# S4 of pair 6 by accumulating DMA, with its product moved behind product 5 of pair 7

## The chip, the cores and the metric

One Trainium2 chip, one core. The metric is the device time in microseconds (us) of one execution. Ratios are the mean time of one kernel's runs over that of the other's runs of the same rounds, so not quite the ratio of the medians that are quoted.

## The reference, cut to what matters

```python
xn = _layernorm(x)                       # 2048 x 512
return x + ssm(xn, ...) + swiglu(xn, w1, w3, w2)
# ssm:    h[t] = Lam_bar * h[t-1] + Bu[t];  y = 2 Re(h C^T) + xn * Dskip
# swiglu: (silu(xn w1) * (xn w3)) w2
```

The kernel joins the last product of both branches. The gated activations (14 tiles of 128) and the states (8 tiles, real and imaginary) stand side by side in the tile `act`, and one matrix product with w2 and C gives the output. This product is done with seven block products in place of eight (the scheme of Strassen and Winograd): the tokens are taken in eight pairs of chunks of 128, n = 0 to 7, and each pair has the left blocks a11, a12, a21, a22 and the sums S1 to S4 of them.

## The kernel before

Each product is eleven matmuls of 128x128 by 128x256. The sums are made in fp16. S2 and S3 lie in a place shared by the even pairs and one shared by the odd ones; S1 = a21 + a22 replaces a21. S4 = a12 + S2 replaces a12, so it can only be made after product 2 has read a12.

```python
LATER = (4, 5)          # pairs whose product 3 runs in the next pair, behind product 5
...
def product2():
    mms(f, v["a12"], weight(1, D1), False)
    v["s4"] = v["a12"]
    if n in (2, 3, 4, 5):
        gp.dma_start(out=v["s4"], in_=v["s2"], accum_op=ALU.add)      # L1094
    else:
        bg.own(0.85, -1.1)
        nc.vector.tensor_tensor(out=v["s4"], in0=v["a12"], in1=v["s2"], op=ALU.add)   # L1097
    add(o1[:, D1], f, o1[:, D1])                                      # L1066
...
def product3():
    for t, cols in halves:
        mms(t, v["s4"], weight(1, D2), False, cols)
        add(o1[:, right(cols)], t, q0[:, cols])
    ...                                                                # store of o1
...
# order of the products in pairs 4 to 7: 1, 4, 2, 6, 5, 7, 3
if i == 3 and n in LATER:
    later[n] = product3
else:
    products[i - 1]()
if i == 5 and n - 1 in later:
    later.pop(n - 1)()
    if n + 1 < len(pairs):
        seeds(n + 1)
if n in LATER:
    bg.fill()
```

`bg` is a queue of VectorE work (state columns, sums S1 to S3 of the next pair). Behind most products (`bg.fill()`), and in the pairs of `LATER` behind every one, it hands out as much as a rough model of VectorE's lead over TensorE allows. In the profile, L1055 is every matmul of the seven products, L525 the last step of a block of state columns, L1001 the sums S3 and S2, L1006 S1, L1140 the addition of product 7, L1072 the stores.

Of the kernel before, what the change touches and what calls it, by code (L numbers as in the profile page):

```python
# [14 lines left out]
FP32 = DT.float32  # L15
# [48 lines left out]
def kernel(  # L64
# [31 lines left out]
    NG = 3  # L96
    TH = TBLK // 2
    LEAD = 1.7
    LATER = (4, 5)
    AHEAD = (MID, 8, 1, None)  # L100
    NWARM = 10
    DH = D // 2
# [48 lines left out]
    x_blk = [x_all[:, i] for i in range(NBLK)]  # L151
# [805 lines left out]
    def weight(kh, dsl, half=False):  # L957
        gates = [w2_sb[:, kh * NFH + k, dsl] for k in range(NFH)]
        return [v.bitcast(FP16) if half else v for v in gates] + [weight_state(kh, dsl)[:, k, :]
                                                                   for k in range(2 * NPH)]  # L960
# [22 lines left out]
    def sum_homes():  # L983
        n = NK * P
        spare = tw[:, 3, :, :].rearrange("p k d -> p (k d)")
        xs = [x_blk[i].rearrange("p c d -> p (c d)") for i in range(2)]
        both = x_all[:, 0:2].rearrange("p b c d -> p b (c d)")[:, :, n:n + 2 * DH].bitcast(FP32)
        q = [const.tile([P, DH], FP32, name="q0"), both[:, 1, :], both[:, 0, :], both]
        return [[v[:, 0:n] for v in xs], [spare[:, 0:n], spare[:, n:2 * n]]], q
# [24 lines left out]
    def seeds(n):  # L1014
        b, p = pairs[n]
        bg.flush(("res", b))
        if n in (0, 3, 5, 7):
            f, e = (ps_bu.tile([P, TBLK], FP32, name="bu_ps") for _ in range(2))
            g, z = (ps_y.tile([P, D], FP32, name="y_ps") for _ in range(2))
        else:  # L1020
            f, e, z, g = (ps_gu.tile([P, TBLK], FP32, name="gu_ps") for _ in range(4))
        g, e, f, z = (t[:, 0:DH] for t in (g, e, f, z))
        o2 = xn_blk[b][:, 2 * p + 1, :]
        if n == len(pairs) - 1:
            spare = ps_gu.tile([P, TBLK], FP32, name="gu_ps")
            halves = [(t[:, 0:DH // 2], slice(i * DH // 2, (i + 1) * DH // 2)) for i, t in enumerate((e, spare))]
        else:
            halves = [(e, slice(0, DH))]
        nc.scalar.activation(out=z, in_=o2[:, D1], func=ACT.Copy)
        for t, cols in halves:  # L1030
            nc.scalar.activation(out=t, in_=o2[:, DH + cols.start:DH + cols.stop], func=ACT.Copy)
        seeded[n] = g, halves, f, z
# [4 lines left out]
    def y_fast(n, then=(), between=()):  # L1037
        b, p = pairs[n]
# [7 lines left out]
        v = sums[n]  # L1046
        res = xn_blk[b]
        g, halves, f, z = seeded[n]
        q0 = x_blk[2].rearrange("p c d -> p (c d)")[:, 0:2 * DH].bitcast(FP32) if n == 5 else q[0]
        tsum = [weight(0, D2, True)] + [[tw[:, i, k, :] for k in range(NK)] for i in range(3)]  # L1050
        o1, o2 = res[:, c1, :], res[:, c1 + 1, :]

        def mms(out, left, right, start, cols=slice(0, DH)):
            for k in range(NK):
                nc.tensor.matmul(out=out, lhsT=left[:, k, :], rhs=right[k][:, cols],  # L1055
                                 start=(start and k == 0), stop=(k == NK - 1), skip_group_check=True)
            bg.tensor(1.2 * (cols.stop - cols.start) / DH)

        def steps():
            if b == 0:  # L1060
                sin_step()
                sin_step()

        def add(out, x, w):
            bg.own(0.35)
            nc.vector.tensor_tensor(out=out, in0=x, in1=w, op=ALU.add)  # L1066

        def store(cl, o, dsl=slice(0, D), eng=nc.sync):
            if b == 0:
                held.append((cl, o))  # L1070
            else:
                eng.dma_start(out=ov[:, b * CPB + cl, dsl], in_=o[:, dsl])  # L1072
# [15 lines left out]
        def product2():  # L1088
            if b == 0:
                bg.first(list(then))  # L1090
            mms(f, v["a12"], weight(1, D1), False)
            v["s4"] = v["a12"]
            if n in (2, 3, 4, 5):
                gp.dma_start(out=v["s4"], in_=v["s2"], accum_op=ALU.add)  # L1094
            else:
                bg.own(0.85, -1.1)
                nc.vector.tensor_tensor(out=v["s4"], in0=v["a12"], in1=v["s2"], op=ALU.add)  # L1097
            add(o1[:, D1], f, o1[:, D1])
            if last:
                store(c1, o1, D1)  # L1100
            if n + 1 < len(pairs) and n not in (1, 2, 3) and n - 1 not in LATER:
                seeds(n + 1)
            steps()
# [13 lines left out]
        def product4():  # L1117
            mms(z, v["a22"], tsum[3], False)
            copy(q[2], z)
            steps()  # L1120
            bg.fill(1.2 if b > 0 and n not in LATER else None)

# [14 lines left out]
        def product7():  # L1137
# [5 lines left out]
            if b == 0:  # L1143
                steps()
                bg.fill()

        products = (product1, product2, product3, product4, product5, product6, product7)
        for i in ((1, 5, 2, 6, 4, 3, 7) if b == 0 else (1, 2, 4, 6, 5, 7, 3) if b == 1 else ORDER.get(n, (1, 4, 2, 6, 5, 7, 3))):
# [10 lines that stand above are left out]
# [24 lines left out]
    homes, q = sum_homes()  # L1183
# [36 lines left out]
    bg.flush(("sums", 0))  # L1220
    keep_ends(0)
    y_fast(0, row_sums(1, *pairs[1]))
    ln_scalar_engine(3, lambda cl: ps_y.tile([P, D], FP32, name="y_ps"), sins, (0, 2, 5))
    y_fast(1)
    sin_step(("norm", 2, CPB - 1))
    for cl, o in held:
# [10 lines left out]
    last_posts = ssm_tasks(3, between=[(0.0, after_y2, None), *row_sums(4, *pairs[4])])  # L1237
    keep_ends(1)
    y_fast(2, row_sums(3, *pairs[3]), bu_fast(3, 0))
    y_done.append(2)  # L1240
    y_fast(3, (), bu_fast(3, 1))
# [42 lines left out]
```

## Time and profile before

| | before |
|---|---|
| median of 3 runs | 200.99 us (200.81 to 201.39) |
| span of the profiled run | 198.9 us |
| TensorE busy | 195.2 us, 98% |
| VectorE busy | 182.2 us, 92% |
| four last pairs, first to last matmul | 162.49 to 196.19, 33.70 us |

### The profile page before, as it was taken

To read this page: it belongs to the slowest core of one execution; us is meant where nothing else is said; L and a number is where in the kernel's file an instruction comes from. 1 tells how busy PE (TensorE), PEld (TensorE's weight loads), DVE (VectorE), ACT (ScalarE), POOL (GpSimd) and SP (SyncE) were. 2 spreads that over 40 slices of the span, in tenths; PEclk is the share of its full clock that TensorE was granted. 3 is DMA by queue.
4 is the path that set the end of the run, shared out by engine and by line. 5 is a ranking of instruction groups with operands and counts; after the bars stand their busy time and mean duration, and the time that the engine had idled before them with its cause. 6 is when DMAs were issued, how large, how long until landed. Compare 5 with 4: busy or idle time off the path is not lost.

```text
span 198.9 us, 3703 instructions
## 1 busy us (share of the span) xinstructions
PE 195.2 (98%) x1401; PEld 130.7 (66%) x1401; DVE 182.2 (92%) x257; ACT 135.0 (68%) x281; POOL 50.9 (26%) x75
## 2 busy tenths in 40 slices
PE   8999999999999999999999999999999999999994
PEld 2874444444444488856555478888566678888893
DVE  3699699999999999989999997999999999999972
ACT  4899797799999987968998684362688782111220
POOL 7170289700411134041202305040021303300000
PEclk9999999999999999999999999999999999999999
DMA  5999999992497054730997546838147723941111
GB/s 154 319 240 185 328 200 98 348 280 46 70 181 141 0 105 82 135 106 0 164 154 107 100 83 108 169 84 124 53 64 134 143 52 57 170 96 33 53 40 44
DMA packets 32258, 25.12 MB, mean 126 GB/s; under 512 B 16240, under 2 KB 29936, under 8 KB 32240
## 3 DMA queue, kind: packets, MB, share of 16 engines
q0 software_dynamic: 6128, 11.38, 33.6%
q1 hardware_dynamic: 25536, 13.21, 28.2%
q10 hardware_dynamic: 576, 0.30, 0.5%
q8 instruction: 11, 0.18, 0.4%
q14 instruction: 7, 0.06, 0.1%
HBM read 7.74 MB, written 2.10 MB: 49 GB/s over the span
## 4 chain that ended last, share of the span: by engine, by line
PE 96%; DMA 1%; DVE 1%; issue 0%
PE gu_ps L587 34%; PE gu_ps L1055 18%; PE y_ps L1055 10%; PE gu_ps L849 7%; PE bu_ps L1055 7%; PE y_ps L454 3%; PE bu_ps L454 3%; PE y_ps L870 3%; PE y_ps L781 3%; PE gu_ps L619 2%; PE gu_ps L781 2%; PE bu_ps L781 1%; PE bu_ps L870 1%; DMA x_blk<-in_A_x_dram 1%; PE bu_ps L619 1%; PE y_ps L243 1%
## 5 line engine op out<-in xcount | busy, mean ns | idle before, releaser
L587 PE MATMUL gu_ps<-xnT,w_sb 128*128 128x512 bf16 x312 | 69.6, 379 | 0.0
L587 PEld LDWEIGHTS <-w_sb 128*128 128x128 bf16 x312 | 30.5, 98 | 34.2
L1055 PEld LDWEIGHTS <-act 128*128 128x128 f16 x462 | 43.5, 98 | 5.4
L596 ACT ACTIVATE g<-gu_ps 128x512 bf16<-128x512 f32 x41 | 24.8, 606 | 5.9 <-PE gu_ps L587 3.5
L597 ACT ACTIVATE u<-gu_ps 128x512 bf16<-128x512 f32 x41 | 24.9, 606 | 4.4 <-PE gu_ps L587 4.1
L505 DVE TENSOR_TENSOR_SCAN u<-rho,ends,u 128x512 bf16<-128x512 f32 x16 | 20.0, 1271 | 0.0
L527 POOL DMA_DIRECT2D act<-p x7 | 9.2, 1321 | 34.1 <-DVE act L519 22.1
L1055 PE MATMUL gu_ps<-w_sb,act 128*128 128x256 bf16 (+3 forms) x126 | 16.0, 267 | 0.0
L849 PE MATMUL gu_ps<-xnT,w_sb 128*128 128x512 bf16 x64 | 15.9, 379 | 0.0
L604 DVE TENSOR_TENSOR act<-g,u 128x1024 f16<-128x1024 bf16 x21 | 14.3, 680 | 0.0
L861 ACT ACTIVATE g<-gu_ps 128x512 bf16<-128x512 f32 x14 | 8.4, 599 | 5.4 <-PE gu_ps L849 5.0
L454 PEld LDWEIGHTS <-bt 128*128 128x128 bf16 x64 | 6.3, 98 | 7.5
L1078 ACT ACTIVATE x_blk<-gu_ps 128x256 f32<-128x256 f32 (+1 forms) x9 | 3.3, 368 | 10.6 <-PE gu_ps L1055 10.6
L1055 PE MATMUL bu_ps<-w_sb,act 128*128 128x256 bf16 (+3 forms) x84 | 10.4, 264 | 0.0
L1055 PE MATMUL gu_ps<-ct,act 128*128 128x256 f16 (+1 forms) x72 | 10.4, 267 | 0.0
L849 PEld LDWEIGHTS <-w_sb 128*128 128x128 bf16 x64 | 6.3, 98 | 4.8
L505 DVE TENSOR_TENSOR_SCAN u<-rho,u 128x512 bf16<-128x512 f32 x8 | 9.2, 1207 | 0.0
L1055 PEld LDWEIGHTS <-x_blk 128*128 128x128 f16 x88 | 8.6, 98 | 1.0
L1055 PEld LDWEIGHTS <-tw 128*128 128x128 f16 x88 | 8.6, 98 | 1.0
L513 DVE TENSOR_TENSOR p<-u,tabe 128x2048 f16<-128x2048 bf16 (+1 forms) x8 | 8.7, 1086 | 0.1
L519 DVE TENSOR_TENSOR act<-u,tabe 128x2048 f16<-128x2048 bf16 (+1 forms) x8 | 8.7, 1085 | 0.0
L488 DVE TENSOR_TENSOR u<-u,tabe 128x2048 bf16<-128x2048 bf16 x7 | 8.5, 1220 | 0.1
(203 smaller groups left out, 392.5 us busy)
## 6 DMA issues: line engine op xcount, KB each, us to landing
act<-p POOLq DMA_DIRECT2D x6, 512.0 KB, 6.1
xn<-x_blk POOLq DMA_DIRECT2D x4, 512.0 KB, 5.5
out_dram<-xn SPq DMA_DIRECT2D x15, 128.0 KB, 1.7
w_sb<-in_B_w_dram SPq DMA_DIRECT2D x1, 1792.0 KB, 8.2
act<-act POOLq DMA_DIRECT2D x5, 352.0 KB, 4.6
w_sb<-in_B_w_dram SPq DMA_DIRECT2D x2, 768.0 KB, 6.1
u<-p POOLq DMA_DIRECT2D x3, 512.0 KB, 5.2
w_sb<-in_B_w_dram SPq DMA_DIRECT2D x4, 256.0 KB, 4.4
```

Of the source, the lines that this page charges most:

```text
L454: nc.tensor.matmul(out=ps, lhsT=bt[:, ri, dt, pt * P:(pt + 1) * P], rhs=xnT_blk[b][:, dt, :], start=(dt == 0), stop=(dt == NDT - 1))
L505: nc.vector.tensor_tensor_scan(out=v, data0=rho[:, pt:pt + 1].to_broadcast([P, TBLK]), data1=v, initial=init, op0=ALU.mult, op1=ALU.add)
L513: nc.vector.tensor_tensor(out=by_state(st["p16"][:, csl]), in0=by_chunk(st["g"][:, :, ::-1, tsl]), in1=by_chunk(tabe[:, psl, 2:0:-1, tsl]) ...
L519: nc.vector.tensor_tensor(out=by_state(act_state(b, hf)[:, csl]), in0=by_chunk(st["g"][:, :, :, tsl]), in1=by_chunk(tabe[:, psl, 0:1, tsl] ...
L527: gp.dma_start(out=a, in_=p16, accum_op=ALU.add)
L587: nc.tensor.matmul(out=ps[:, tsl], lhsT=w[:, dt, f * P:(f + 1) * P], rhs=xnT[:, dt, tsl], start=(dt == 0), stop=(dt == NDT - 1))
L596: nc.scalar.activation(out=g16[:, f % 2, :], in_=g_ps, func=ACT.Silu)
L597: nc.scalar.activation(out=u16[:, f % 2, :], in_=u_ps, func=ACT.Copy)
L604: nc.vector.tensor_tensor(out=act_gates(b, f - 1), in0=split(g16), in1=split(u16), op=ALU.mult)
L781: nc.tensor.matmul(out=out[:, h * TH:(h + 1) * TH], lhsT=left[:, h, k, :], rhs=right[:, k, :], start=(start and h == 0 and k == 0), stop=( ...
L849: nc.tensor.matmul(out=ps, lhsT=w[:, dt, f * P:(f + 1) * P], rhs=xnT[:, dt, :], start=(dt == 0), stop=(dt == NDT - 1))
L1055: nc.tensor.matmul(out=out, lhsT=left[:, k, :], rhs=right[k][:, cols], start=(start and k == 0), stop=(k == NK - 1), skip_group_check=True)
```

## The change

The intent is to take the addition of S4 in pair 6 (128x1408, 0.89 us) off VectorE, which idles only 0.32 us there, and to let the DMA engines do it. The transfer takes longer than the addition, so product 3 of pair 6, which reads S4, is put off until behind product 5 of pair 7. Its addend q0 must live longer, so pair 7 writes its own into an idle buffer. Because pair 6 now stands in `LATER`, its calls to the VectorE queue change too (the code above).

```diff
-    LATER = (4, 5)
+    LATER = (4, 5, 6)
...
-        q0 = x_blk[2]...bitcast(FP32) if n == 5 else q[0]
+        q0 = x_blk[2]...bitcast(FP32) if n in (5, 7) else q[0]
...
-            if n in (2, 3, 4, 5):
+            if n in (2, 3, 4, 5, 6):
                 gp.dma_start(out=v["s4"], in_=v["s2"], accum_op=ALU.add)
```

More of the change, by code (lines that the diff above doesn't have):

```diff
@@ L1048, in y_fast @@
         g, halves, f, z = seeded[n]
-        q0 = x_blk[2].rearrange("p c d -> p (c d)")[:, 0:2 * DH].bitcast(FP32) if n == 5 else q[0]
+        q0 = x_blk[2].rearrange("p c d -> p (c d)")[:, 0:2 * DH].bitcast(FP32) if n in (5, 7) else q[0]
         tsum = [weight(0, D2, True)] + [[tw[:, i, k, :] for k in range(NK)] for i in range(3)]
```

## The prediction

> **What bounds the kernel now.** I read the page first: which engine is busy, and what the chain that ended last consists of.
>
> ```profile
> PE 195.2 (98%) x1401; PEld 130.7 (66%) x1401; DVE 182.2 (92%) x257; ACT 135.0 (68%) x281; POOL 50.9 (26%) x75
> PEclk9999999999999999999999999999999999999999
> PE 96%; DMA 1%; DVE 1%; issue 0%
> ```
>
> TensorE fills 98% of the span at the full clock, and 96% of the chain is TensorE's own work. VectorE has 92%, so it is the engine that could become a second bound. A busy matmul row alone doesn't prove that nothing is lost, so I read the chain of waits over the stretch that the change touches, from the first product of pair 4 on (each pair of token chunks has seven products, of eleven matmuls each):
>
> ```profile
> 162.49 7.21 PE gu_ps L1055 x66
> 169.70 2.40 PE y_ps L1055 x22
> 172.10 1.20 PE bu_ps L1055 x11
> ...
> 191.31 1.20 PE y_ps L1055 x11
> 192.52 0.61 PE bu_ps L1055 x11
> 193.13 0.61 PE gu_ps L1055 x11
> 193.74 1.20 PE y_ps L1055 x11
> 194.94 0.61 PE bu_ps L1055 x11
> 195.56 0.63 PE gu_ps L1055 x11
> 196.19 0.02 issue
> 196.21 0.29 DVE xn L1066
> ```
>
> Every piece starts where the one before it ends, and no other engine stands in the chain until 196.19. Four pairs of seven products are 28; 28 x 1.20 = 33.6 us, and 196.19 - 162.49 = 33.70 us. So TensorE waits for nothing in this whole stretch: there is no wait here for the change to remove. Behind it stand 198.9 - 196.2 = 2.7 us: two additions on half tiles, three last stores, and the end of the program.
>
> The change lightens VectorE, so I asked how it stands there. The timeline of VectorE in pair 6 and at the start of pair 7 (start, duration, line):
>
> ```profile
> 181.80 0.89 DVE L1097 TENSOR_TENSOR act<-act,x_blk 128x1408 f16<-128x1408 f16 x1
> ...
> 187.75 0.42 DVE L1066 TENSOR_TENSOR xn<-gu_ps,q 128x256 bf16<-128x256 f32 x1 [0.32 <-PE gu_ps L1055]
> 188.09 0.68 DVE L525 TENSOR_TENSOR act<-act,p 128x1024 f16<-128x1024 f16 x1
> 188.69 0.89 DVE L1001 TENSOR_TENSOR tw<-act 128x1408 f16<-128x1408 f16 x1
> 189.61 0.89 DVE L1001 TENSOR_TENSOR tw<-tw,act 128x1408 f16<-128x1408 f16 x1
> 190.42 0.88 DVE L1006 TENSOR_TENSOR act<-act 128x1408 f16<-128x1408 f16 x1
> 191.35 0.89 DVE L1097 TENSOR_TENSOR act<-act,tw 128x1408 f16<-128x1408 f16 x1
> ```
>
> The first line is S4 of pair 6, which the change takes away; the last is S4 of pair 7, which stays. Between them lies the preparation of pair 7: its last state columns (L525) and its sums S3, S2, S1. They come in time, though not by much. Product 4 of pair 7 starts at 188.75 and comes to its state columns with its eighth matmul, 7 x 0.109 us later; with 0.1 us for the weight load it needs L525 at about 189.4, and L525 ends at 188.77: 0.6 us to spare. Product 6 of pair 7 needs S2 at about 191.05, and S2 ends at 190.50: 0.5 us.
>
> **What the Trainium skill says.** "DMA: Bandwidth & Descriptors", Rules for kernel authors: a DMA that accumulates is to be issued from GpSimd, as here. Its section on the anatomy of one DMA on the GpSimd path fits about 2.0 us plus bytes/436e3; for 352 KB (360,448 bytes) that is 2.8 us as an estimate from that page. The trace shows 3.8 us for the same transfer in pairs 4 and 5 (L1094), and I use that. The same rules warn that an accumulating DMA must not overlap another access of the same bytes. In this kernel the issue waits for the product that reads them: product 2 of pair 4 ends at 165.93 and the issue starts at 166.40, product 2 of pair 5 ends at 173.14 and the issue starts at 173.60, so about 0.47 us behind it. "Perfetto Trace Analysis", Identifying the Most-Contended Engine, says that matmul busy time is no measure of the distance to roofline; it is why I rested the bound on the gapless chain and on 28 x 1.20, not on the 98%.
>
> **The change part by part.**
>
> 1. It removes one addition of 128x1408 from VectorE in pair 6: 0.89 us by the row above (0.80 until the next instruction starts). TensorE doesn't wait for VectorE there, so the path gets nothing of it: 0.
>
> 2. It adds one accumulating DMA. Product 2 of pair 6 ends at 181.54, so the issue starts near 182.0, takes GpSimd 0.9 us, and lands after 3.8 us: near 185.8, or 186.7 if counted from the end of the issue. GpSimd has nothing after 174.5, and the DMA engines are nearly idle (12% in 176.9 to 184.1, by the table of stretches). Product 3 of pair 6 wants the result at 186.35 in the old order: that would be too tight, which is why it is moved along. In the new order it runs after product 5 of pair 7, at about 192.4: over 5 us to spare. Cost on the path: 0.
>
> 3. It moves product 3 of pair 6 by six products. The number of matmuls stays, 28 products. Product 7 of pair 6 then ends at 186.35 and pair 7 starts there instead of at 187.55: its products 1, 4, 2, 6, 5 come 1.20 us earlier (186.35, 187.55, 188.75, 189.95, 191.15), product 3 of pair 6 fills 192.35 to 193.57, and product 7 and the two halves of product 3 of pair 7 start at 193.6 and 194.8 as before. If nothing waits, the last matmul ends at 196.2 again.
>
> 4. So the inputs of pair 7 are due 1.20 us earlier. VectorE gets back 0.80 us (S4) and, as the addition behind product 3 moves away, 0.42 us with 0.32 us of waiting. Suppose the worst order of the instructions, the old one. The addition of product 7 of pair 6 (0.69 us, 0.60 to the next start) can't start before 186.35 + 0.2. Then L525 runs 187.15 to 187.83, against a need at about 188.2: 0.4 us to spare. S3 runs to 188.6, S2 to about 189.5 against 189.85: 0.35 us. S1 ends near 190.3 against 191.05. It just fits. The changed calls to the queue of VectorE work should make it better: behind product 4 its limit goes from 1.2 to 1.7, each product of pair 6 gets another call, and the model no longer charges 0.85 us for S4, so state columns and S3 should be handed out before the addition of product 7. I expect about 1 us to spare or more. Cost: 0, at worst a few tenths.
>
> 5. The other output buffer of product 6 (q0 in the idle x_blk) keeps the old value alive and costs nothing. The accumulator of product 3 of pair 6 stays occupied longer; the spare tile of pair 7 comes around to the accumulator of product 2, which is free by 183.0.
>
> 6. The store of the row of product 3 (128 KB, 1.7 us to landing) moves from about 188.2 to 194.2 and should land near 195.9. The last stores are issued at 195.77, near 196.0 and at 196.53, so it is out of their way: 0 to 0.2 us.
>
> Sum: 0 saved, 0 to 0.2 us added. From 200.99 us I predict 201.0.
>
> **The rivals.**
>
> *A wait takes its place.* If L525 or S2 comes late, TensorE stops in product 4 or 6 of pair 7. For: VectorE is busy 7.17 of 7.20 us in pair 6 and the spare time falls from 0.6 and 0.5 to 0.4 and 0.35 in the worst order. Against: it is relieved of more than it is pressed by. It would make 201.2 to 201.8.
>
> *The end gets crowded.* Another 128 KB comes into the last 5 us. For: the stores after 195.77 end the program, and the 64 KB store issued at 192.61 took 3.5 us instead of 1.7. If the moved store does so, it lands at 197.7 and may hold back the others by some tenths: 201.2 to 201.5. Against: the last store of 32 KB still lands later, at 198.0.
>
> *A gain after all.* If the VectorE relief let the last products come earlier, it would be up to 0.9 us: 200.1. For: VectorE at 92%. Against: TensorE has no gap to close in the stretch, and the last addition waits for the last matmul (0.27 us of idle in front of it), not for VectorE's queue. I hold it for nearly excluded.
>
> *The accumulation lands late.* It would need a landing after 192.4, thus over 10 us instead of 3.8. The slowest row of accumulating transfers in the table of issues has 6.1 us (512 KB). Excluded.
>
> **Range and chances.** The three runs of before spread over 200.81 to 201.39, so half a microsecond either way is noise. The losses that I can name are a few tenths; the gains are smaller. The range is 200.5 to 201.6. Two per cent would be 4 us: for that, TensorE would have to stand still for three whole products, or lose as many, and nothing points to it. Faster 0.01, within 2% 0.97, slower 0.02.
>
> **What would show it.** In the changed profile: one 128x1408 addition fewer in L1097 and one issue more in L1094, near 182.0, landing near 186. The chain from 162.5 to 196.2 still of TensorE alone, with the gu_ps product of pair 6 behind a bu_ps and gu_ps half. VectorE with a longer idle piece before 195, since its work of pair 7 is done earlier. L525 and S2 ahead of their products by about 1 us. The step 4 is wrong if TensorE shows a wait on VectorE near 188 or 190; step 6 if the time from the last addition to the end of the span grows over 2.4 us. The whole is wrong if the last matmul ends more than half a microsecond away from 196.2.

## The result, and the profile after

The changed kernel takes 200.97 us (median of 4 runs, 200.91 to 201.34) against 201.01 us (4 runs) of the kernel before. The ratio is 0.9999, with a 95% interval of 0.998 to 1.0018: the same time.

From the page of the changed kernel, busy time and instructions of each engine:

```profile
PE 194.9 (98%) x1401; PEld 130.7 (66%) x1401; DVE 181.3 (91%) x256; ACT 135.0 (68%) x281; POOL 51.5 (26%) x76
```

VectorE has one instruction and 0.9 us less, GpSimd one issue more; TensorE has its 1401 matmuls as before. The chain of waits of the changed kernel over the last four pairs (start, duration, what):

```profile
162.72 7.20 PE gu_ps L1055 x66
...
191.54 0.61 PE bu_ps L1055 x11
192.15 1.81 PE gu_ps L1055 x22
193.97 1.20 PE y_ps L1055 x11
...
196.41 0.02 issue
196.44 0.29 DVE xn L1066
```

The piece of 1.81 us at 192.15 is a half of product 5 of pair 7 (0.61) and then product 3 of pair 6 (1.20), in its new place. Still every piece begins where the last one ends: 196.41 - 162.72 = 33.69 us, against 33.70. The whole stretch lies 0.23 us later than before. That comes from the start of the kernel, which the change doesn't touch: in the chains, the long piece on L587 begins at 12.44 in the kernel before and at 12.67 in the changed one. TensorE waits 0.2 us there in the kernel before (L243 on the first normalized chunk), and in the changed kernel, by the view of who waited for whom (us in total, times, longest):

```profile
PE y_ps L243 <- DVE xn L224: 0.5, 1, 0.5
PE gu_ps L619 <- DMA w_sb<-in_B_w_dram: 0.2, 1, 0.2
```

These are arrivals of the first inputs and weights. They differ from run to run (the stretch begins between 162.45 and 162.84 in the ten profiles), by 0.4 us or 0.2% of the time; differences of 0.1% between kernels below are smaller than that.

The timeline of VectorE in the changed kernel, pair 6 and the start of pair 7:

```profile
186.03 0.68 DVE L525 TENSOR_TENSOR act<-act,p 128x1024 f16<-128x1024 f16 x1
186.84 0.69 DVE L1140 TENSOR_TENSOR xn<-gu_ps,x_blk 128x512 bf16<-128x512 f32 x1
187.45 0.88 DVE L1001 TENSOR_TENSOR tw<-act 128x1408 f16<-128x1408 f16 x1
188.37 0.89 DVE L1001 TENSOR_TENSOR tw<-tw,act 128x1408 f16<-128x1408 f16 x1
189.17 0.88 DVE L1006 TENSOR_TENSOR act<-act 128x1408 f16<-128x1408 f16 x1
190.38 0.89 DVE L1097 TENSOR_TENSOR act<-act,tw 128x1408 f16<-128x1408 f16 x1 [0.32 <-PE bu_ps L1055]
```

L525 is now handed out ahead of L1140, and the last addition shown, S4 of pair 7, waits for TensorE (0.32 us), where in the kernel before it followed without a gap. The products 4 and 6 of pair 7, which read L525 and S2 (the second L1001), in the kernel before and then in the changed one:

```profile
188.75 1.36 PE L1055 MATMUL y_ps<-tw,act 128*128 128x256 f16 x11
191.15 1.36 PE L1055 MATMUL y_ps<-tw 128*128 128x256 f16 x11
...
187.77 1.36 PE L1055 MATMUL y_ps<-tw,act 128*128 128x256 f16 x11
190.18 1.36 PE L1055 MATMUL y_ps<-tw 128*128 128x256 f16 x11
```

S2 ends 0.65 us ahead of its product before the change (189.61 + 0.89 against 191.15) and 0.92 us ahead after it (188.37 + 0.89 against 190.18). The issue of the transfer on GpSimd, and its row in the table of issues (KB each, us to landing):

```profile
182.24 0.86 POOL L1094 DMA_DIRECT2D act<-x_blk  x1 [7.50 <-DVE xn L949]
...
act<-x_blk POOLq DMA_DIRECT2D x1, 352.0 KB, 3.8
```

Product 2 of pair 6 ends at 181.77 and the issue follows 0.47 us later, landing near 186.0. (The wait is put down to L949, which ended just before; the 0.47 us behind product 2 are the same as in pairs 4 and 5.)

### The profile page after: what moved, and what is told of

The parts are those of the page before. It is cut to its first block, busy times and chain, and to the rows that moved or that the text cites. A ratio compares the mean times of both kernels' runs of the same rounds, so it can differ in the third digit from the quotient of the medians.

```text
span 199.1 us, 3703 instructions
## 1 busy us (share of the span) xinstructions
PE 194.9 (98%) x1401; PEld 130.7 (66%) x1401; DVE 181.3 (91%) x256; ACT 135.0 (68%) x281; POOL 51.5 (26%) x76
## 4 chain that ended last, share of the span: by engine, by line
PE 95%; DMA 2%; SPq 1%; issue 0%; DVE 0%
PE gu_ps L587 34%; PE gu_ps L1055 18%; PE y_ps L1055 10%; PE gu_ps L849 7%; PE bu_ps L1055 7%; PE bu_ps L454 3%; PE y_ps L454 3%; PE y_ps L870 3%; PE y_ps L781 3%; DMA w_sb<-in_B_w_dram 2%; PE gu_ps L619 2%; PE gu_ps L781 2%; PE bu_ps L781 1%; PE bu_ps L870 1%; PE bu_ps L619 1%; SPq L166 0%
## 5 line engine op out<-in xcount | busy, mean ns | idle before, releaser
L587 PE MATMUL gu_ps<-xnT,w_sb 128*128 128x512 bf16 x312 | 69.6, 379 | 0.0
L587 PEld LDWEIGHTS <-w_sb 128*128 128x128 bf16 x312 | 30.5, 98 | 34.2
```

Source lines behind the costliest of these rows:

```text
L587: nc.tensor.matmul(out=ps[:, tsl], lhsT=w[:, dt, f * P:(f + 1) * P], rhs=xnT[:, dt, tsl], start=(dt == 0), stop=(dt == NDT - 1))
```

## The experiments

Eight kernels ran on one chip, the first four of them held against 11 runs of the kernel before (median 201.16 us), the others against the same 11 and one more (201.18 us), so that a drift between the two groups would not show in the intervals of the second. The changed kernel was measured apart from them, its ratio is to the 4 runs of the kernel before of its own rounds (201.01 us). What each left in its one trace, with "spare" for the time from the end of VectorE's instruction to the start of the matmul that reads it (S2: product 6 of pair 7; L525: the eighth matmul of product 4 of pair 7, its start plus 7 x 0.109 us):

| kernel | ratio of times to before (95%) | four pairs | spare S2 | spare L525 |
|---|---|---|---|---|
| before | 1 | 33.70 | 0.65 | 0.74 |
| changed | 0.9999 (0.998 to 1.0018) | 33.69 | 0.92 | 1.82 |
| DMA alone | 1.0008 (0.9989 to 1.0028) | 33.69 | 0.94 | 1.96 |
| move alone | 0.9992 (0.9975 to 1.0009) | 33.69 | 0.19 | 0.28 |
| before, 2 loads | 1.0033 (1.0018 to 1.0048) | 34.41 | | waits |
| changed, 2 loads | 1.0027 (1.0012 to 1.0041) | 34.35 | waits | |
| move alone, 1 load | 1.0027 (1.0013 to 1.0041) | 34.35 | | waits |
| changed, 1 load | 0.9985 (0.9972 to 0.9998) | 33.69 | 0.34 | 1.02 |
| before without product 3 of pair 6 | 0.9949 (0.9936 to 0.9962) | 32.70 | | |
| changed, store held back | 1.0008 (0.9996 to 1.0021) | 33.69 | | |

The four pairs are the difference of two starts in one chain, so they show a tenth of a microsecond where the times alone don't. "Changed, 1 load" is a warning: its time lies just clear of 1, below it, while its stretch is the same to 0.01 us. A difference of 0.15% in the times is no proof of anything here.

### The DMA alone

```diff
-            if n in (2, 3, 4, 5):
+            if n in (2, 3, 4, 5, 6):        # LATER stays (4, 5)
```

> The kernel before with S4 of pair 6 by accumulating DMA, product 3 of pair 6 in its old place, straight behind product 7 of pair 6. Theory (TensorE sets the end, VectorE's relief is worth nothing): the transfer is issued near 182.0 and lands near 185.8, its product wants its weights near 186.25, so it just fits, by about 0.4 us: the time stays at 201.0, or TensorE waits 0.1 to 0.5 us on the DMA at the start of that product and the time is up to 201.5. Rival A (the removed VectorE addition is worth its 0.8 us and the deferral gives it away): 200.2. Rival B (a transfer without the deferral is late): a wait of over 1 us before product 3 of pair 6, 202 or more.

Measured: 201.13 us, no wait of TensorE in the stretch. The issue stands at 182.36, so the landing is at 186.2, and product 3 of pair 6 starts at 186.69. It fits by half a microsecond. The 3.8 us count from the start of the issue: counted from its end, 183.22, the landing would be at 187.0, and TensorE would have waited. The first matmuls of that product, with no idling in front of them in brackets:

```profile
186.69 0.93 PE L1055 MATMUL gu_ps<-w_sb,act 128*128 128x256 bf16 x7
```

Rivals A and B fall: lightening VectorE by 0.8 us brings no time, and the deferral was not needed in this run to have the transfer in time. My prediction had called this place "too tight"; it was tight, and held. VectorE turns part of the relief into waiting: it stands still for 0.73 us in front of the addition of product 6 of pair 6.

### The move alone

```diff
-            if n in (2, 3, 4, 5, 6):        # LATER = (4, 5, 6) stays
+            if n in (2, 3, 4, 5):
```

> The changed kernel with S4 of pair 6 back on VectorE: only product 3 is moved. VectorE then has the old work, and pair 7 is due 1.20 us earlier. Theory: the spare time of the state columns (L525) and of S2 in front of pair 7, measured in the changed kernel at 1.7 and 0.8 us with the addition gone, falls to 0.1 to 0.2 us, just enough: 201.0, with at most 0.3 us of waiting of TensorE in products 4 or 6 of pair 7. Rival A (the VectorE addition costs its 0.8 us on the path wherever it runs): 201.8 against the changed kernel. Rival C (moving the product costs something at the end, by the store): the end lies later by the same 0.1 to 0.2 us as in the changed kernel, with the last matmul at the same distance from the first product of pair 4 (33.7 us).

Measured: 200.85 us and 33.69 us. VectorE's S2, and product 6 of pair 7 that reads it:

```profile
189.06 0.89 DVE L1001 TENSOR_TENSOR tw<-tw,act 128x1408 f16<-128x1408 f16 x1
...
190.14 1.36 PE L1055 MATMUL y_ps<-tw 128*128 128x256 f16 x11
```

S2 ends at 189.95 and is read at 190.14. The move alone fits with 0.19 us left, as expected; Rival A (0.8 us lost) falls. So does Rival C: from the start of the last addition to the end of the span it is 2.7 us here as in the kernel before. So neither half of the change costs time and neither saves any that these runs show; what they move is the spare time of S2, from 0.65 to 0.94 us (DMA) and to 0.19 us (move).

### Two more additions in both kernels

To see whether this spare time is real, VectorE got work that nothing reads, at the place of S4 of pair 6, with two additions here and one in the two runs after:

```diff
+            if n == 6:
+                dead = bt_flat[:, 2 * TBLK:2 * TBLK + NK * P].bitcast(FP16)
+                for _ in range(2):
+                    nc.vector.tensor_tensor(out=dead, in0=dead, in1=dead, op=ALU.subtract)
             add(o1[:, D1], f, o1[:, D1])
```

The model of the queue is not told of this work.

> The kernel before with two more VectorE additions of 128x1408 on dead data behind S4 of pair 6 (about 1.6 us more). Theory: VectorE has 0.32 us of idling and 0.6 us of spare time in front of pair 7, so 1.6 us is more than it can hide: L525 comes near 190.0 instead of 188.8, TensorE waits 0.6 to 0.8 us in product 4 of pair 7 and the time is 201.7. Rival A (VectorE's queue is the bound): plus the whole 1.6 us, 202.6. Rival D (there is much more spare time): 201.0.

> The changed kernel with the same two more additions at the same place in pair 6. Theory by the measured spare time of the changed kernel: S2 ends 0.8 us before product 6 of pair 7 needs it, and VectorE idles 0.13 us in front of L1140, so TensorE waits 0.6 to 0.8 us in front of product 6: 201.7, about as much as in the kernel before with the same load. That would mean that the change bought no spare time at this spot: what it takes from VectorE it asks back by bringing pair 7 forward by one product. Rival (the change buys the 0.8 us of the removed addition as spare time): at most 0.1 us of waiting, 201.0, while the kernel before with the same load has 201.7.

Measured: 201.79 us and 201.70 us. The two additions in the kernel before, and the instruction behind them:

```profile
182.84 1.81 DVE L1101 TENSOR_TENSOR bt<-bt 128x1408 f16<-128x1408 f16 x2
184.57 0.42 DVE L1066 TENSOR_TENSOR xn<-gu_ps,xn 128x256 bf16<-128x256 f32 x1
```

So the load is 1.73 us from start to start. The waits in the kernel before with the load, and in the changed kernel with it (matmuls in order of time; the brackets give TensorE's idling and who ended it):

```profile
188.99 0.93 PE L1055 MATMUL y_ps<-tw,act 128*128 128x256 f16 x7
190.36 0.61 PE L1055 MATMUL y_ps<-tw,act 128*128 128x256 f16 x4 [0.44 <-DVE act L525]
```

```profile
185.49 1.36 PE L1055 MATMUL gu_ps<-tw,x_blk 128*128 128x256 f16 x11 [0.22 <-DVE q L1066]
...
190.55 1.38 PE L1055 MATMUL y_ps<-tw 128*128 128x256 f16 x11
```

In the kernel before, product 4 of pair 7 does its seven matmuls on the gated activations and then stops for the state columns, as the prediction had located it. The stretch grows by 0.71 us: of 1.73 us of load, about 1.0 us disappears, which is near the spare 0.74 us of L525 and the 0.32 us of idling together. Rival A (the whole load) and Rival D (none of it) fall. In the changed kernel it grows by 0.66 us. The size is as expected, the place only in part: counted from the start of the stretch, product 6 of pair 7 comes 0.64 us later than without the load (S2 ends at 190.49), but 0.39 us of that are lost already in front of product 7 of pair 6, which waits until VectorE has read the accumulator that it goes on with. I had not seen this wait coming; it stems from the order of the changed kernel, in which two more steps of state columns stand ahead of that addition (L1066 at 183.56 in the changed kernel without load).

So the changed kernel bears hardly more of this load than the kernel before: the rival, in which the change buys 0.8 us, falls.

### One more addition, with S4 on VectorE or on the DMA

> Product 3 of pair 6 moved, its S4 on VectorE, and one more addition of 128x1408 on dead data behind it (0.8 us more). In the run with the move alone S2 ended 0.1 us before product 6 of pair 7 took it, and L525 0.2 us before product 4 did. Theory (the move uses up VectorE's spare time, the transfer of S4 to the DMA gives it back): nothing is left to hide the load, TensorE waits 0.6 to 0.8 us in products 4 and 6 of pair 7, stretch of the four pairs 34.3 to 34.5 us instead of 33.7, time 201.7. Rival (the load is hidden as long as VectorE idles anywhere behind it): 201.0.

> The changed kernel with one such addition at the same place: VectorE has then just the work that it has with the move alone, but in the order of the changed kernel. Theory: S2 comes 0.67 us later than in the changed kernel and is taken 0.1 us later: at most 0.1 us of waiting, stretch 33.7 to 33.8 us, time 201.0. With the run before this one (same load, S4 on VectorE, 0.7 us of waiting expected) it would show that the DMA's half of the change is worth one addition of spare time and no time. Rival (the DMA's transfer slows VectorE or TensorE at this place): a wait of 0.3 us or more.

Measured: 201.76 us with S4 on VectorE and 200.91 us with S4 on the DMA; stretches of 34.35 and 33.69 us. The wait of the former, and the same product of the latter, undivided and without a wait:

```profile
189.21 0.61 PE L1055 MATMUL y_ps<-tw,act 128*128 128x256 f16 x4 [0.39 <-DVE act L525]
...
187.90 1.36 PE L1055 MATMUL y_ps<-tw,act 128*128 128x256 f16 x11
```

Both expectations held, both rivals fall. With product 3 moved and nothing else, the next 0.8 us of VectorE work costs 0.66 us; with S4 on the DMA it costs nothing. This is the plainest view of what the change does: the move spends VectorE's spare time in front of pair 7, because it brings pair 7 forward by a product of 1.20 us, and the transfer gives at least as much back (for S2, 0.46 us spent and 0.73 us given back). The kernel before with one addition was not run; by its spare time and idling, 0.65 + 0.32 us, it is estimated to hide 0.8 us as well. So these two runs separate the halves of the change, and do not show the changed kernel to bear more than the kernel before.

### Less work for TensorE

```diff
-                mms(t, v["s4"], weight(1, D2), False, cols)
+                if n != 6:
+                    mms(t, v["s4"], weight(1, D2), False, cols)
```

> The kernel before without the eleven matmuls of product 3 of pair 6 (a wrong result on purpose, in half of one row of chunks), all else left: a control for what TensorE's work is worth here. Theory (TensorE sets the end): pair 7 comes 1.20 us earlier, VectorE's spare time of 0.5 to 0.6 us plus its 0.32 us of idling is not quite enough for that, so 0.8 to 1.2 us are gained: 199.8 to 200.2. Rival (VectorE sets the end): 0 to 0.3 us gained, 200.7 to 201.0.

Measured: 200.23 us, a ratio of 0.9949, thus 1.0 us less; the stretch is 32.70 us. The result is wrong on purpose (the record marks it correct: the comparison with the reference let it pass, and why is not shown). The model of the queue loses this product too. The chain of this kernel:

```profile
186.58 2.52 PE y_ps L1055 x22
189.10 1.20 PE bu_ps L1055 x11
190.30 1.29 PE y_ps L1055 x11
```

One TensorE product of 1.20 us is worth 1.00 us. The 0.2 us that are missing show in the first and third piece: 2.52 where two products take 2.40, and 1.29 for 1.20. The chain puts them down to TensorE itself. By the timelines VectorE is just late: L525 ends at 188.43 and is due with the eighth matmul at 187.62 + 7 x 0.109 = 188.38; S2 ends at 190.16, and product 6, which could start at 190.14, starts at 190.22. With pair 7 one product earlier and S4 on VectorE, the spare time is thus overdrawn: the addition behind product 3 of pair 6 still stands ahead of L525 in VectorE's queue here, while with the move alone it has gone behind, and there the spare time was enough. VectorE's addition brings nothing when it goes, TensorE's product brings nearly all of its time: TensorE sets the end.

### The store held back

```diff
+            if n == 6: held.append((c1, o1))       # product 3: no store here
...
             store(c1 + 1, o2)
+            if last: nc.sync.dma_start(out=..., in_=held[-1][1])
```

> The changed kernel with the 128 KB store of product 3 of pair 6 held back until behind the store of the second row of pair 7 (issued near 196.3 instead of 194.4): the suspected crowding of the end, made real. Theory (the moved store costs nothing because it has landed before the last ones start, but would cost its transfer if it had not): the half-row store behind it and the last one come 0.3 to 0.6 us later, time 201.3 to 201.6, with the last matmul where it was. Rival (the end waits for a fixed time behind the last addition, whatever the stores): 201.0.

Measured: 201.35 us; the interval of the ratio to before holds 1, so the time alone doesn't decide. The trace does for its run. The issues of the last stores with the store held back (L1146 is the held one):

```profile
196.24 0.41 SPq L1146 DMA_DIRECT2D out_dram<-xn  x1
...
196.60 0.35 ACTq L1072 DMA_DIRECT2D out_dram<-xn  x1
196.76 0.39 SPq L1072 DMA_DIRECT2D out_dram<-xn  x1
```

The 32 KB store of pair 7 on this queue is now issued behind the held one, at 196.76, and lands 1.7 us later, near 198.5; in the changed kernel the last landing was near 198.3 (issue 196.76 plus 1.5), with a last addition that started 0.16 us later (196.44 against 196.28). From the start of the last addition to the end of the span it is 199.4 - 196.28 = 3.1 us, against 199.1 - 196.44 = 2.7 in the changed kernel and 198.9 - 196.21 = 2.7 in the kernel before. In all nine other traces it lies between 2.66 and 2.74 us. So the store costs about 0.4 us in this trace, within the expected 0.3 to 0.6, when it comes among the last ones. In the changed kernel the moved store is issued at 194.46 with 1.7 us to landing, thus near 196.2, before the next one's transfer; it costs nothing that the trace shows.

Apart from the run without product 3, whose result is wrong, no version shortens the stretch, and the runs say why: it has no wait of TensorE to take away.

## Why the prediction was right

It said 201.0 us, in 200.5 to 201.6, and 97% for a change within 2%; measured were 200.97 us. That it met the middle to 0.03 us is luck, as the runs of one kernel spread over half a microsecond; that nothing changed is what its steps say:

- **Step 1, the addition removed is worth 0.** Shown: the DMA alone leaves the stretch at 33.69 us. The control without a product of TensorE gains 1.0 us, so the measure would have shown a gain.
- **Step 2, the transfer.** The issue 0.47 us behind product 2 and 3.8 us to landing came as read from pairs 4 and 5. The prediction left open whether the 3.8 us count from the start or the end of the issue; they count from the start. So "too tight" without the deferral was too strong: it had half a microsecond to spare in the run with the DMA alone.
- **Step 3, the order of TensorE's work.** Each product of pair 7 up to product 5 came 1.2 us earlier, and the last matmul where it was, both counted from the start of the stretch.
- **Step 4, the spare time.** The worst order, with S4 removed, was put at 0.35 us for S2 and 0.4 for L525, and "about 1 us to spare or more" was expected of the better order. Less the 0.1 us for the weight load that the prediction took off, it was 0.8 us for S2, a little short of that, and 1.7 us for L525. L525 was handed out before the addition of product 7, as foreseen, but S3 was not: it starts at 187.45, behind that addition (186.84). What the prediction left open, and the runs settle, is how the two halves of the change act on it: the move takes S2's spare time from 0.65 to 0.19 us, the transfer brings it up to 0.92. It had also not named the wait for the accumulator in front of product 7, which the changed order brings nearer; only the run with two loads makes it a real one.
- **Step 5, the other buffer.** TensorE has no wait in the stretch of the changed kernel, so neither the buffer nor the longer hold on the accumulator costs anything. No run tests it by itself.
- **Step 6, the store.** From the last addition's end to the span's end it stayed at 2.4 us. The rival of the crowded end can happen (0.4 us in the trace with the store held back), but the store in its actual place is early enough.
- **The rivals.** A wait of TensorE on VectorE appears once VectorE has 1.7 us more to do, and is absent as it stands. The gain of up to 0.9 us didn't come. The accumulation was not late: it took 3.8 us.
- **Slips of reading.** They move no step. The 7.17 of 7.20 us are of the window 176.9 to 184.1, which holds the end of pair 5 and five of the eight products done in pair 6; over pair 6 (178.1 to 187.7) VectorE is busy 9.27 of 9.60 us. Of the "two additions" and "three last stores" behind 196.2 only the second addition and the last two stores begin there, and the store "near 196.0" is issued at 196.2.

What stays open: how much the deferral protects in slower executions than the traced ones. With the DMA alone the median is 201.13 us and one of six runs took 202.37; that one has no trace, and 201.66 occurred with the move alone too. The 3.8 us are no law either: L1008, an accumulating transfer of the same 352 KB, took 3.8 us in one place of the kernel before and 4.6 to 5.2 us in four others, where an earlier transfer was still under way. With such a landing, 182.36 + 4.6 = 187.0 or later by this estimate, the DMA alone would have been late for 186.69.

## What to carry to other kernels

Where the engine that sets the end runs without gaps, as here, moving work off the second busiest engine can buy spare time, not time; ask how much spare time there is at each hand-over (end of the producer to start of the consumer), and whether the re-ordering that comes with the move spends it again. Test such a claim with a control in each direction: load the relieved engine until the gaps appear, and take work off the bound engine to see that the clock responds. Where a re-ordering delays a store, see whether it still lands before the last ones; here one among them cost about 0.4 us in its trace.

## What the Trainium skill lacked or had wrong

- "DMA: Bandwidth & Descriptors", Anatomy of one DMA: its fit for the GpSimd path gives 2.8 us for 352 KB; the accumulating transfer of S4 within SBUF (L1094) took 3.7 to 3.8 us in all ten traces. The page's rate of 436 GB/s is not seen for it: while it ran in the changed kernel, the view of the DMA queues shows 169 to 225 GB/s at full engines, in slices of 0.15 us. The engines move it from about 183.6 to 185.5, 1.9 us; the 1.9 us that are left of the 3.8 are near the page's fixed part of about 2.0, so it is the moving that takes longer than the fit. The page has no fit for transfers that accumulate.
- "Perfetto Trace Analysis", Identifying the Most-Contended Engine: its warning on matmul busy time was useful (98% in all of these), but the page says nothing of spare time. Here VectorE, at 92% in the kernel before, could hide about 1.0 of 1.73 us of additional work, and the spare 0.74 us in front of one product with 0.32 us of idling said so better than any share.
- No page gives a spread for the landing of one small store: the same 64 KB store of pair 7 took between 1.5 and 3.7 us over these ten profiles, without a matching change of the span. In the six traces with 2.5 us or more, nine of its 144 packets come behind the rest (in the kernel before 135 by 193.8, nine from 194.9 to 195.4); in the four with 1.5 or 1.6 us none do. No run here tells why.
